# Masking a chunk's last attention unit on VectorE, with its values one step ahead

## The chip, the cores and the metric

The kernel runs on one core of a Trainium2 chip. The metric is the device time of one execution in microseconds, from the median of several runs. The core has five engines that each work through their own queue in order: TensorE (PE, with its weight loads PEld), VectorE (DVE), ScalarE (ACT), GpSimd (POOL) and SyncE (SP), which issues all DMAs of this kernel.

## The reference

Top-k attention for 64 heads, followed by a two-layer MLP with a leaky ReLU:

```python
batch, n_heads, seq, head_dim = (8, 8, 576, 64)
scores = scale * np.matmul(q, k.transpose(0, 1, 3, 2))
kth = np.partition(scores, -32, axis=-1)[..., -32:-31]
scores = np.where(scores >= kth, scores, -1000000000.0)
attn = np.exp(scores - np.max(scores, axis=-1, keepdims=True))
attn = attn / (np.sum(attn, axis=-1, keepdims=True) + 1e-09)
x = np.matmul(attn, v)          # (B,H,S,D) -> (B*S, H*D) = (4608, 512)
h = x @ w_in                    # (512, 2048)
g = np.maximum(0.01 * h, h)
out = g @ w_out                 # (2048, 512)
```

For each query the 32 largest of 576 scores are kept, the others are masked, and what is kept is exponentiated, normalised and multiplied with the values.

## The kernel before, in words

**Units.** The attention is cut into 144 units. A unit is 128 query rows (or two half blocks of 64) of a pair of heads, so it has two score matrices of 128x576. The units of four head pairs together fill 128 tokens. The tokens are cut into chunks for the MLP: two of 128 tokens, then seventeen of 256. Units 0 to 3 make chunk 0, units 4 to 7 chunk 1, units 8 to 15 chunk 2, and so on, eight units each.

**What happens to a unit.** `scores` (L191): PE computes both score matrices into two PSUM tiles `psc0` and `psc1`, ACT copies them into `s_sb`. `top_k` (L209): DVE finds the 32 largest of each row in four rounds of eight, after it has folded the row into maxima and minima of pairs; the round's results go to `tops`, the first entry of the first round is the maximum, the last entry of the last round the threshold. `mask` (L228): POOL computes the bias for the exponential and adds a large negative number to all scores below the threshold. `exponents` (L237): ACT takes the exponential and sums each row into `z`. `sums` (L241): ACT adds 1e-9, giving `ze`. `reciprocals` (L245): DVE. `normalize` (L249): ACT. `transpose` (L252): ACT splits the 32-bit words into two planes of 16 bits (`split`), two DMAs store them to DRAM (`apart`), and a transposing DMA reads them back as `wT`, which has three buffers. `weigh_values` (L276) multiplies with the values on PE into `po`, `keep_values` (L290) copies into the MLP's input `x` on ACT.

**The order.** It is written out by hand, in a loop of steps (L416). In step s DVE does the top k of unit s in four slots (`slot()`); POOL masks unit s-1 and ACT exponentiates it; unit s-2 gets its reciprocals, normalisation and transpose, in the step's second quarter. At every even step the scores of units s+2 and s+3 are made and the values of two units (s-4 and s-3) are weighed, so `values_at(n)` (L356) is n+3, rounded up to an even number. When the values of a chunk's last unit have been weighed, the chunk is ready (`attended`, L373), and its MLP is dealt out in pieces over seven places of each step until the next chunk gets ready (`mlp_steps` and `slot_budget`, L337 and L379). Each MLP piece of the first layer (`ph`) is closed by a Prelu on ACT (L313); three PSUM tiles rotate for both layers. The second layer (`pz`) needs ACT only for one copy per 128 tokens (L326).

**The lead-in.** The MLP weights arrive as 64-bit words in 16 pieces and are rounded to float32 by ACT, DVE and PE together (`round_weights`, L103); a piece goes through three stages in three turns of the loop at L400. The raw pieces lie in the three buffers of the pool `raws`. The scores of units 0 and 1 are issued in this loop too, in the turn of piece 14.

Of the kernel before, what the change touches and what calls it, by code (L numbers as in the profile page):

```python
# [8 lines left out]
F32 = mybir.dt.float32  # L9
U32 = mybir.dt.uint32  # L10
U16 = mybir.dt.uint16
BF16 = mybir.dt.bfloat16
AF = mybir.ActivationFunctionType
ALU = mybir.AluOpType
# [5 lines left out]
def kernel(  # L20
# [13 lines left out]
    nc = tc.nc  # L34
    NPAIR, P, S = qT.shape
# [3 lines left out]
    ROUNDS = TOPK // 8  # L39
    SLOPE = 0.01  # L40
    LOWEST = -3.4028234663852886e38
    SCALE = float(D) ** -0.5
# [5 lines left out]
    WCH = 1024  # L48
# [10 lines left out]
    raws = ctx.enter_context(tc.tile_pool(name="raws", bufs=3))  # L59
    work = ctx.enter_context(tc.tile_pool(name="work", bufs=2))  # L60
    small = ctx.enter_context(tc.tile_pool(name="small", bufs=5))
# [18 lines left out]
    NPIECE = 2 * HP * DFF // WCH  # L80
# [13 lines left out]
    def load_weights(n):  # L94
        if n >= NPIECE:
            return
        if not AS_WORDS:
            nc.sync.dma_start(piece(n), weights[n])
            return
        raw_of[n] = raws.tile([P, WCH, 4], U16, name="raw")  # L100
        nc.sync.dma_start(raw_of[n].rearrange("p n w -> p (n w)"), weights[n])
# [51 lines left out]
    def load_qk(pi):  # L153
        qt = loads.tile([P, S], F32, name="qt")
        kt = loads.tile([P, S], F32, name="kt")
        nc.sync.dma_start(qt, qT[pi])
        nc.sync.dma_start(kt, kT[pi])
        qk_of[pi] = qt, kt

    def load_v(pi):  # L160
        v_of[pi] = loads.tile([P, NKC, 2, D], F32, name="vt", bufs=LOADED_V)
        nc.sync.dma_start(v_of[pi], vk[pi])
# [28 lines left out]
    def scores(u):  # L191
        ps = [ps_sc.tile([P, 2, 512], F32, name=f"psc{i}") for i in range(2)]
        for n in range(0, len(u.parts), 2):
            for half in range(2):
                for i, pi, side, r0 in u.parts[n:n + 2]:
                    qt, kt = qk_of[pi]
                    d = slice(side * D, (side + 1) * D)
                    nc.tensor.matmul(  # L198
                        ps[i][r0:r0 + u.rows, half, 0:HS],
                        qt[d, u.q0:u.q0 + u.rows],  # L200
                        kt[d, half * HS:(half + 1) * HS],
                        start=True, stop=True,
                    )
        u.both = work.tile([P, 2, S], F32, name="s_sb", bufs=5)
        u.s = [u.both[:, i, :] for i in range(2)]
        for i in range(2):
            nc.scalar.copy(u.s[i].rearrange("p (h n) -> p h n", h=2), ps[i][:, :, 0:HS])  # L207

    def top_k(u):  # L209

        u.tops = small.tile([P, 2, ROUNDS, 8], F32, name="tops")
        pairs = work.tile([P, 2, 2, HS], F32, name="pairs", bufs=1)
        for n, op in enumerate((ALU.max, ALU.min)):
            nc.vector.tensor_tensor(pairs[:, :, n, :], u.both[:, :, 0:HS], u.both[:, :, HS:S], op)  # L216
        for r in range(ROUNDS):
            rest = [pairs[:, i, 0, :] if r < ROUNDS // 2 else
                    pairs[:, i, :, :].rearrange("p n h -> p (n h)") for i in range(2)]
            for i in range(2):  # L220
                nc.vector.max(out=u.tops[:, i, r, :], in_=rest[i])  # L221
            if r + 1 < ROUNDS:
                for i in range(2):
                    nc.vector.match_replace(out=rest[i], in_to_replace=u.tops[:, i, r, :],  # L224
                                            in_values=rest[i], imm_value=LOWEST)
            yield

    def mask(u, i):  # L228
        if i == 0:
            u.nbias = small.tile([P, 2], F32, name="nbias")  # L230
            u.z = small.tile([P, 2], F32, name="z")
            nc.gpsimd.tensor_scalar(u.nbias, u.tops[:, :, 0, 0], -SCALE, None, ALU.mult)  # L232
        pen = work.tile([P, S], F32, name="pen", bufs=1)
        nc.gpsimd.tensor_scalar(pen, u.s[i], u.tops[:, i, ROUNDS - 1, 7:8], MASKED, ALU.is_lt, ALU.mult)  # L234
        nc.gpsimd.tensor_tensor(u.s[i], u.s[i], pen, ALU.add)  # L235
# [5 lines left out]
    def sums(u):  # L241
        u.ze = small.tile([P, 2], F32, name="ze")
        nc.scalar.activation(u.ze, u.z, AF.Copy, bias=1e-9, scale=1.0)  # L243

    def reciprocals(u):  # L245
        u.rz = small.tile([P, 2], F32, name="rz")
        nc.vector.reciprocal(u.rz, u.ze)  # L247

    def normalize(u, i):  # L249
        nc.scalar.activation(u.s[i], u.s[i], AF.Copy, bias=0.0, scale=u.rz[:, i:i + 1])  # L250

    def transpose(u):  # L252


        pairs = u.both.rearrange("p i n -> p (i n)").bitcast(U16).rearrange("p (n h) -> p n h", h=2)
        apart = halves.tile([P, 2, 2 * S], U16, name="apart")
        for h in range(2):
            split = work.tile([P, 2 * S], U16, name="split", bufs=2)
            nc.scalar.copy(split, pairs[:, :, h])  # L259
            nc.sync.dma_start(apart[:, h, :], split)  # L260
        u.wT = work.tile([P, 2 * NKC - 1, P], F32, name="wT", bufs=3)
        nc.sync.dma_start_transpose(out=u.wT.bitcast(U16), in_=apart.rearrange("p h n -> (p h) n"))
# [89 lines left out]


    LAG = 3

    def values_at(n):  # L356

        return n + LAG + (n + LAG) % 2

    steps = units  # L360

    def unit(n):
        return steps[n] if 0 <= n < len(steps) else None
# [15 lines left out]
    def slot_budget(s):  # L379

        after = [at for at, _ in ready_at if at >= s]
        until = after[0] if after else s
        return backlog[0] / ((until + 1 - s) * SLOTS)
# [3 lines left out]
    with tc.manual_schedule():  # L387
        last = {p: n for n, u in enumerate(steps) for p in u.pairs}

        def load_more(s):  # L390

            for of, load, n, lag in ((qk_of, load_qk, LOADED, -2), (v_of, load_v, LOADED_V, LAG + 1)):
                while len(of) < NPAIR and (len(of) < n or last[len(of) - n] + lag <= s):
                    load(len(of))


        for n in range(3):
            load_weights(n)
        rounding = {}
        for n in range(NPIECE + 2):  # L400
            for i in (n, n - 1, n - 2) if AS_WORDS else ():
                if 0 <= i < NPIECE:
                    if i == n:
                        rounding[i] = round_weights(i)
                    next(rounding[i], None)
            load_weights(n + 3)
            if 6 <= n < 6 + HP:
                load_qk(n - 6)
            elif n == NPIECE - 2:
                for u in steps[0:2]:  # L410
                    scores(u)
            elif n == NPIECE - 1:
                load_v(0)
                load_v(1)

        for s in range(len(steps) + LAG + 1):  # L416
            cur, old, older, new = unit(s), unit(s - 1), unit(s - 2), ()
            if s % 2 == 0:
                new = [u for u in steps[s + 2:s + 4] if u]
            picks = top_k(cur) if cur else iter(())  # L420
            budget = slot_budget(s)

            def slot():
                next(picks, None)

            slot()
            if old:
                mask(old, 0)
                mask(old, 1)
            mlp_steps(budget)  # L430
            slot()
            if older:
                reciprocals(older)
                normalize(older, 0)
                normalize(older, 1)
            mlp_steps(budget)
            if old:
                exponents(old, 0)
            if older:
                transpose(older)  # L440
            slot()
            mlp_steps(budget)
            mlp_steps(budget)
            slot()
            mlp_steps(budget)
            if old:
                exponents(old, 1)
                sums(old)
            for u in new[:1]:
                scores(u)  # L450
            if s % 2 == 0:
                po = ps_po.tile([P, 2, P], F32, name="po")
                for values in (weigh_values, keep_values):
                    for n, u in enumerate((unit(s - LAG - 1), unit(s - LAG))):
                        if u:
                            values(u, po[:, n, :])
                attended(s)
            for u in new[1:]:
                scores(u)
            budget = slot_budget(s + 1)  # L460
            mlp_steps(budget)
            mlp_steps(budget)
            load_more(s)
        mlp_steps(1e9)
# [58 lines left out]
```

## Time and profile before

| | |
|---|---|
| median of three runs | 1515.37 us (1514.73 to 1516.42) |
| profiled execution, span | 1512.57 us, 1510.8 us |
| PE busy | 1423.4 us (94%) |
| DVE busy | 1330.6 us (88%) |
| ACT busy | 1117.7 us (74%) |
| POOL busy | 1078.1 us (71%) |
| mask on POOL, L234 and L235 | 288 times each, 2214 and 1411 ns |
| exponential, L238 | 288 times, 768 ns |
| split, L259 | 288 times, 1144 ns |
| tensor_tensor of 128x576 on DVE, L216 | 288 times, 780 ns |

Times in the profile are microseconds from the start of the span. An engine's busy time is what its instructions took; a bracket such as [6.15 <-DMA wT<-apart] behind an instruction is the idle time before it and what ended that. "x20" is the number of instructions that a line merges. A line number is that of the kernel before.

### The profile page before, as it was taken

Reading aid. Unit: us, or ns where it says so; the run is one execution under the profiler, and the core shown is the slowest. Engines: PE = TensorE matmul, PEld = TensorE weight load, DVE = VectorE, ACT = ScalarE, POOL = GpSimd, SP = SyncE. Lnnn points to the kernel's source line nnn. Section 1 sums busy time; section 2 is a strip of 40 time slices with the busy share of each in tenths; the row PEclk is TensorE's granted clock in tenths of the full one; section 3 lists DMA queues with packets and bytes.
Section 4 is the critical chain, followed back from the end, with each engine's and each line's share of the span. In section 5 each row is a group of like instructions: output and inputs, shape, how many; then the busy total and the mean of one; then the engine's idle time right before and its main releaser. Section 6 shows DMA issues by size and latency. Waiting matters only on the chain.

```text
span 1510.8 us, 24439 instructions
## 1 busy us (share of the span) xinstructions
PE 1423.4 (94%) x8190; PEld 946.7 (63%) x8192; DVE 1330.6 (88%) x3421; ACT 1117.7 (74%) x2141; POOL 1078.1 (71%) x726
## 2 busy tenths in 40 slices
PE   5736978999999999999999999999999999999998
PEld 2214655767676766676767666767666666676774
DVE  6799999999899999899999998999999989999600
ACT  7846787878787877787878787878787777787720
POOL 0058878887777877777778787878887878788700
PEclk9966999999999999999999999999999999999999
DMA  7714466555665455545764455645665455554510
GB/s 284 283 31 126 131 173 167 162 140 144 183 158 154 128 158 163 169 128 153 181 169 136 140 159 166 170 133 145 188 162 146 133 159 154 152 136 140 141 50 14
DMA packets 399294, 227.05 MB, mean 150 GB/s; under 512 B 343360, under 2 KB 343360, under 8 KB 397120
## 3 DMA queue, kind: packets, MB, share of 16 engines
q1 hardware_dynamic: 399168, 225.49, 53.4%
q8 instruction: 64, 1.05, 0.3%
q14 instruction: 62, 0.51, 0.1%
HBM read 46.14 MB, written 94.37 MB: 93 GB/s over the span
## 4 chain that ended last, share of the span: by engine, by line
PE 83%; DVE 10%; ACT 4%; DMA 1%; issue 1%; POOL 0%; DVEq 0%; ACTq 0%; POOLq 0%
PE pz L319 32%; PE ph L307 31%; PE psc L198 10%; PE po L283 10%; DVE tops L221 4%; DVE pairs L224 3%; DVE pairs L216 1%; ACT split L259 1%; DMA wT<-apart 1%; DMA raw<-in_weights_dram 1%; ACT s_sb L238 1%; ACT s_sb L250 0%; DVE scale L144 0%; ACT s_sb L207 0%; ACT wT L121 0%
## 5 line engine op out<-in xcount | busy, mean ns | idle before, releaser
L234 POOL TENSOR_SCALAR pen<-s_sb,tops 128x576 f32<-128x576 f32 x288 | 637.5, 2214 | 234.4 <-DVE tops L221 197.4
L221 DVE MAX8 tops<-pairs 128x8 f32<-128x288 f32 (+1 forms) x1152 | 636.1, 591 | 0.0
L307 PE MATMUL ph<-x,w_in 128*128 128x256 f32 (+1 forms) x2432 | 515.4, 371 | 6.4 <-ACT gT L313 6.4
L319 PE MATMUL pz<-w_out,gT 128*128 128x512 f32 x1152 | 506.8, 595 | 1.3 <-ACT gT L313 1.3
L307 PEld LDWEIGHTS ph<-x,w_in 128*128 128x128 f32 x2432 | 440.5, 191 | 86.5 <-issue 21.5
L224 DVE MATCH_REPLACE8 pairs<-tops,pairs 128x288 f32<-128x288 f32 (+1 forms) x864 | 460.3, 538 | 0.0
L235 POOL TENSOR_TENSOR s_sb<-s_sb,pen 128x576 f32<-128x576 f32 x288 | 406.5, 1411 | 24.1
L319 PEld LDWEIGHTS pz<-w_out,gT 128*128 128x128 f32 x1152 | 216.0, 190 | 265.9 <-issue 263.5
L259 ACT COPY split<-s_sb 128x1152 uint16<-128x1152 uint16 x288 | 315.6, 1144 | 0.0
L207 ACT COPY s_sb<-psc 128x576 f32<-128x576 f32 x288 | 169.2, 639 | 114.1 <-PE psc L198 114.1
L250 ACT ACTIVATE s_sb<-s_sb,rz 128x576 f32<-128x576 f32 x288 | 206.6, 767 | 33.7 <-DVE rz L247 33.6
L238 ACT ACTIVATE s_sb<-s_sb,nbias 128x576 f32<-128x576 f32 x288 | 221.1, 768 | 11.4 <-POOL s_sb L235 11.4
L198 PE MATMUL psc<-kt,qt 64*128 64x288 f32 (+1 forms) x1280 | 198.1, 439 | 28.5 <-ACT s_sb L207 28.4
L216 DVE TENSOR_TENSOR pairs<-s_sb 128x576 f32<-128x576 f32 x288 | 213.6, 780 | 10.2 <-ACT s_sb L238 0.5
L283 PE MATMUL po<-wT,vt 128*64 128x128 f32 (+1 forms) x3200 | 180.5, 269 | 21.1 <-DMA wT<-apart 21.0
L283 PEld LDWEIGHTS po<-wT,vt 128*64 128x64 f32 x3200 | 161.6, 139 | 52.6 <-issue 27.2
L313 ACT ACTIVATE gT<-ph 128x256 f32<-128x256 f32 (+1 forms) x304 | 107.1, 368 | 97.8 <-PE ph L307 97.4
L198 PEld LDWEIGHTS psc<-kt,qt 64*128 64x128 f32 (+1 forms) x1280 | 110.1, 181 | 100.9 <-ACT s_sb L207 37.8
L232 POOL TENSOR_SCALAR nbias<-tops 128x2 f32<-128x2 f32 x144 | 33.4, 232 | 92.3 <-DVE tops L221 79.6
L247 DVE RECIPROCAL rz<-ze 128x2 f32<-128x2 f32 x144 | 22.4, 156 | 70.0 <-ACT ze L243 69.4
L297 ACT COPY x<-po 128x128 f32<-128x128 f32 (+1 forms) x160 | 32.4, 264 | 63.4 <-PE po L283 63.4
L224 DVE MATCH_VALUE_LOAD pairs<-tops,pairs 128x8 f32 x864 | 62.6, 72 | 0.0
(38 smaller groups left out, 312.2 us busy)
## 6 DMA issues: line engine op xcount, KB each, us to landing
apart<-split SPq DMA_DIRECT2D x288, 288.0 KB, 2.1
raw<-in_weights_dram SPq DMA_DIRECT2D x16, 1024.0 KB, 4.9
vt<-in_vk_dram SPq DMA_DIRECT2D x32, 320.0 KB, 3.6
qt<-in_qT_dram SPq DMA_DIRECT2D x32, 288.0 KB, 4.0
kt<-in_kT_dram SPq DMA_DIRECT2D x32, 288.0 KB, 4.2
out_dram<-o_sb SPq DMA_DIRECT2D x36, 256.0 KB, 2.0
wT<-apart SPq DMA_TRANSPOSE x144, 4.6
```

What stands on the lines that cost most here:

```text
L198: nc.tensor.matmul(ps[i][r0:r0 + u.rows, half, 0:HS], qt[d, u.q0:u.q0 + u.rows], kt[d, half * HS:(half + 1) * HS], start=True, stop=True,)
L216: nc.vector.tensor_tensor(pairs[:, :, n, :], u.both[:, :, 0:HS], u.both[:, :, HS:S], op)
L221: nc.vector.max(out=u.tops[:, i, r, :], in_=rest[i])
L224: nc.vector.match_replace(out=rest[i], in_to_replace=u.tops[:, i, r, :], in_values=rest[i], imm_value=LOWEST)
L234: nc.gpsimd.tensor_scalar(pen, u.s[i], u.tops[:, i, ROUNDS - 1, 7:8], MASKED, ALU.is_lt, ALU.mult)
L235: nc.gpsimd.tensor_tensor(u.s[i], u.s[i], pen, ALU.add)
L238: nc.scalar.activation(u.s[i], u.s[i], AF.Exp, bias=u.nbias[:, i:i + 1], scale=SCALE, accum_out=u.z[:, i:i + 1])
L250: nc.scalar.activation(u.s[i], u.s[i], AF.Copy, bias=0.0, scale=u.rz[:, i:i + 1])
L259: nc.scalar.copy(split, pairs[:, :, h])
L283: nc.tensor.matmul(po[side * D:(side + 1) * D, o, :], vt[:, c, side, :], u.wT[:, c + side * NKC if c + 1 < NKC else c, r:r + n], start=(c ...
L307: nc.tensor.matmul(ph[:, 0:n], w_in[c][:, f * P:(f + 1) * P], x[c][:, 0:n], start=(c == 0), stop=(c == HP - 1),)
L319: nc.tensor.matmul(pz[0:m, 0:DMODEL], gT[f][:, r0:r0 + m], w_out[f // 4][:, f % 4, :], start=(f == 0), stop=(f == NFC - 1),)
```

## The change

It concerns the last unit of each of the first five chunks: units 3, 7, 15, 23 and 31, called hurried here. For them the exponentials of all 576 scores, not of the masked ones, are taken on ACT during the unit's own step, as soon as the first round of its top k has given the maximum; they go into a buffer of the pool `raws`, which is free by then. At the head of the next step DVE masks and sums them in one instruction per matrix: (score >= threshold) times exponential, with a row sum. Then the reciprocals, the normalisation and the transpose are issued for the unit before it and for the hurried unit, one after the other, ahead of the step's top k. POOL does nothing for a hurried unit. The values of it and of the unit before are weighed one step earlier, in an odd step, so the chunk is ready one step earlier.

Apart from that, the scores of units 0 and 1 are issued one turn later in the lead-in, in the turn of piece 15.

```diff
+    def hurried_exponents(u):
+        u.nbias = small.tile([P, 2], F32, name="nbias")
+        nc.scalar.activation(u.nbias, u.tops[:, :, 0, 0], AF.Copy, bias=0.0, scale=-SCALE)
+        e = raws.tile([P, WCH, 4], U16, name="raw").rearrange("p n w -> p (n w)").bitcast(F32)
+        u.e = [e[:, i * S:(i + 1) * S] for i in range(2)]
+        for i in range(2):
+            nc.scalar.activation(u.e[i], u.s[i], AF.Exp, bias=u.nbias[:, i:i + 1], scale=SCALE)
+
+    def hurried_masks(u):
+        u.z = small.tile([P, 2], F32, name="z")
+        for i in range(2):
+            nc.vector.scalar_tensor_tensor(
+                out=u.s[i], in0=u.s[i], scalar=u.tops[:, i, ROUNDS - 1, 7:8], in1=u.e[i],
+                op0=ALU.is_ge, op1=ALU.mult, accum_out=u.z[:, i:i + 1])
+        u.ze = small.tile([P, 2], F32, name="ze")
+        nc.vector.tensor_scalar(u.ze, u.z, 1e-9, None, ALU.add)
...
+    HURRIED = {3, 7, 15, 23, 31}
     def values_at(n):
-        return n + LAG + (n + LAG) % 2
+        return n + LAG + (n + LAG) % 2 - ((n | 1) in HURRIED)
...
-            elif n == NPIECE - 2:
+            elif n == NPIECE - 1:
                 for u in steps[0:2]:
                     scores(u)
-            elif n == NPIECE - 1:
+            if n == NPIECE - 1:
                 load_v(0)
                 load_v(1)
...
+            if s - 1 in HURRIED:
+                hurried_masks(old)
+                for u in (older, old):
+                    reciprocals(u)
+                for u in (older, old):
+                    normalize(u, 0)
+                    normalize(u, 1)
+                    transpose(u)
+                old = older = None
+            elif s - 2 in HURRIED:
+                older = None
             slot()
+            if s in HURRIED:
+                hurried_exponents(cur)
...
-            if s % 2 == 0:
+            due = [u for n, u in enumerate(steps) if values_at(n) == s]
+            if due:
                 po = ps_po.tile([P, 2, P], F32, name="po")
                 for values in (weigh_values, keep_values):
-                    for n, u in enumerate((unit(s - LAG - 1), unit(s - LAG))):
-                        if u:
-                            values(u, po[:, n, :])
+                    for n, u in enumerate(due):
+                        values(u, po[:, n, :])
                 attended(s)
```

## The prediction

> **What bounds the kernel now.** I read the page's forty slices first, then the stages, then the timelines of PE, DVE and ACT over the first 260 us.
>
> ```profile
> PE   5736978999999999999999999999999999999998
> DVE  6799999999899999899999998999999989999600
> ```
> PE is short of work in the first seven slices only (one slice is 37.8 us); DVE is full there. The stages say it in numbers (columns: stage, length, then busy time of PE, PEld, DVE, ACT, POOL, and PE clock):
> ```profile
> 80.00:145.00 65.00, 26.62 (x137) 18.29 (x135) 64.55 (x173) 35.96 (x67) 49.95 (x34) 0.56 0.30 84
> 145.00:192.00 47.00, 42.22 (x298) 31.19 (x297) 44.20 (x116) 35.32 (x75) 39.23 (x27) 0.99 0.46 121
> 192.00:255.00 63.00, 50.76 (x393) 34.27 (x394) 61.28 (x161) 50.44 (x106) 50.24 (x35) 0.95 0.65 177
> 410.00:490.00 80.00, 80.00 (x438) 54.62 (x437) 73.99 (x193) 63.56 (x126) 62.80 (x43) 1.00 0.59 151
> 490.00:1440.00 950.00, 949.48 (x5594) 639.04 (x5593) 876.63 (x2282) 739.75 (x1449) 748.01 (x499) 1.00 0.56 152
> ```
> From 255 us to the end PE never rests, so the end moves only by PE idle time that is removed or added early on. Up to there DVE sets the pace: a step of top k takes 8.87 us (rows of L216 below), and DVE waits for nothing but this:
> ```profile
> 113.88 1.45 DVE L216 TENSOR_TENSOR pairs<-s_sb 128x576 f32<-128x576 f32 x2
> 122.68 1.52 DVE L216 TENSOR_TENSOR pairs<-s_sb 128x576 f32<-128x576 f32 x2
> ...
> 154.52 0.17 DVE L247 RECIPROCAL rz<-ze 128x2 f32<-128x2 f32 x1 [0.58 <-ACT ze L243]
> ...
> 192.90 0.17 DVE L247 RECIPROCAL rz<-ze 128x2 f32<-128x2 f32 x1 [2.73 <-ACT ze L243]
> ...
> 223.85 1.45 DVE L216 TENSOR_TENSOR pairs<-s_sb 128x576 f32<-128x576 f32 x2
> ```
> These are the starts of steps 4, 5 and 16. PE in turn waits for the transposed weights of a chunk's last unit (po), and the MLP (ph) starts behind them:
> ```profile
> 138.94 2.40 PE L283 MATMUL po<-wT,vt 128*64 128x128 f32 x20 [6.15 <-DMA wT<-apart]
> 142.20 2.82 PE L198 MATMUL psc<-kt,qt 64*128 64x288 f32 x8 [0.85 <-ACT s_sb L207]
> 144.95 6.23 PE L307 MATMUL ph<-x,w_in 128*128 128x128 f32 x48
> ...
> 249.94 2.40 PE L283 MATMUL po<-wT,vt 128*64 128x128 f32 x40
> 253.00 1.77 PE L198 MATMUL psc<-kt,qt 64*128 64x288 f32 x8 [0.65 <-ACT s_sb L207]
> 254.70 10.65 PE L307 MATMUL ph<-x,w_in 128*128 128x256 f32 x48
> ```
> The first group is unit 3 and chunk 0; the second units 14 and 15 and chunk 2, after which PE is saturated. Unit 3's top k ends at 113.8, its weights are there at 138.9: 25.1 us.
>
> [...]
>
> **The change, part by part.**
> *Mask.* Per hurried unit two DVE passes of 128x576: from 0.71 us each (L216 in pairs)[...]; I take 0.76. With two accumulator reads (about 0.1 each) and ze this is 1.65 us[...]. POOL loses its 7.2 us of L234 and L235; it is not the bound.
>
> *Exponentials early.* ACT gains nbias (0.2) and moves two exponentials (1.44 as a pair) ahead of the normalisation and exponentials of the step. So the sum ze of the unit before comes 1.65 us later.
>
> *Reciprocals first.* In before DVE asks for ze of the unit two back 4.5 us into a step (118.40 in step 4). Now it asks at the head of the step, behind the masks. All of the step's top k queues behind that wait, and by it PE's scores and POOL's masks. This is the price I find decisive. h is what a hurried unit delays DVE:
> - Unit 3: ACT copies scores until 110.24 (109.06+1.18), then exponentials to 111.9, then the old sequence from normalise to ze, 5.3 us (110.14 to 115.43): ze at 117.2. The masks are done at 115.5[...]. Two reciprocals, 0.3: step 4 starts at 117.6, not 113.88. h=3.7.
> - Unit 7: chunk 0's MLP now runs in steps 6 and 7, so ACT also carries its Prelus. Step 6 starts at 135.1, normalise follows the reciprocal at 139.7-140.3, ze of unit 5 at 146.1 (5.8 us as in the rows at 156.38 to 162.15, Prelus in between); two score copies with PE between them to 149.6, two Prelus to 150.4, exponentials to 152.0, normalise to ze again 5.8 with some more Prelus: 158.5. DVE would have been there at 152.8. h=5.7 (5 to 7.5).
> - Unit 15: ACT is free at 220.1 (behind the score copy of 218.86), so by the old rows ze of unit 14 moves from 225.7 to 227.4, 3.6 after the step's start at 223.85; with reciprocals h=3.9.
> - Units 23 and 31: second half of a chunk, where pz needs no Prelu; I take 3.5 each.
>
> *The chain to the weights.* From the reciprocals on: normalise and split of one unit 1.44+2.19, the same of the other: 7.2 us of ACT. SP is in order: the first transpose is issued 2.2 us after its split, holds SP 2.5, the second unit's apart DMAs come behind it, 3.3 us later its transpose, 4.6 to landing. For unit 3: 117.5, splits done 121.1 and 124.7, transposes at 123.3 and 129.3, weights at 133.9. That is 20.1 us after top k's end, 5.0 less than before. wT has three buffers, so unit 7's transpose also waits until PE has weighed unit 4's values, by my count at 168, before the transpose's own time of 170.4 (158.8+11.6); not a new bound, but close.
>
> *Values one step ahead.* Chunk 0's MLP starts at 137 instead of 145, but scores of units 8 and 9 (2.8 each at the slow clock) now stand behind it. What counts is the start of chunk 2, where PE fills up. Step 16 starts at 223.85 + 3.7 + 5.7 - 3.3 (DVE's two waits above, which the shift swallows) = 229.9. Weights of unit 15 at +20.1 = 250.0, po 1.3, copy 0.3: MLP at 251.6. Two scores of step 18 (2.4 us) are still to do, so it compares as 254.0 with 254.7: 0.7 us gained.
>
> *Scores one piece later in the lead-in.* ACT starts on piece 15 2.8 us earlier (71.86 to 69.1), but four score copies and PE's scores now stand ahead of the scale of piece 15 (74.97 to 75.9) and its matmuls: DVE ends at 79.0 instead of 78.6. 0.4 lost, between 1 gained and 1.5 lost.
>
> *Back to the old rhythm.* Chunks 3 and 4 take PE 74.6 us for eight steps (po of 325.28 to 399.86); DVE needs 71 plus h. The chunk after the last hurried unit has nine steps between its values: PE 77.1. PE is done at 251.6+74.6+74.6+77.1 = 477.9. DVE: step 40 at 229.9+213+10.9 (h of 15, 23, 31) = 453.8, weights of unit 39 by the old chain at +25.1 = 478.9. PE waits 1.0.
>
> Sum: -0.7+0.4+1.0 = 0.7 us slower, against the span of 1510.8. The profiled run took 1512.57, the median of the timed ones is 1515.37; I add to the latter: 1516.0.
>
> **Rivals.**
> *Slower: DVE becomes the bound for the hurried chunks.* For: 71+3.5 is already 74.5 against PE's 74.6, and where PE lags, ze waits for PE through ACT's queue (46 waits of 69.4 us in the whole of before). If h of 15, 23 and 31 sum to 16 instead of 10.9, unit 39's weights come at 484, PE waits 6: 1521. It decides from a sum of about 13. Against: in these steps ACT has few Prelus.
> *Faster: the sums are there in time.* If unit 6's sum comes with the masks' end (h=2 at unit 7), chunk 2 starts 4.4 us ahead; with later h summing to 9.9 or less PE doesn't wait at unit 39, and 0.4 goes for the lead-in: 1511.4. For: ACT is 74% busy only; against: its order in steps 6 and 7 as worked out. All waits gone, h=1.9 everywhere, brings step 16 5.6 us forward and shortens its chain by 1.7: 1507.8.
> *The chain is not shortened.* If SP's order costs the whole 5 us (qk loads before the transpose, as at 230 us, where 5 us passed between apart and transpose), chunk 2 is 4 us late: 1520. It is counted with slower.
>
> **How the numbers follow.** No change from before can be told within 0.2%, that is 3.0 us. Level 0.37 (own range 1512.4 to 1518.4), slower 0.35 (1518.4 to 1527), faster 0.28 (1507.8 to 1512.3). The bounds of the parts (h of unit 7 5 to 7.5, lead-in, later h) spread by some 4 us each way, and the rivals by 6; leaving out a tenth at each end gives 1508 to 1525.
>
> **What would show it.** Right: chunk 0's first ph near 137; a DVE wait for ze at the head of steps 4, 8 and 16 of about 2, 4 and 2 us; the pair of transposes some 6 us apart; chunk 2's first ph near 252; a po wait near 478. Wrong: reciprocals there without a wait (faster), masks above 1.4 us each so that they outlast ze, PE idle at each of the chunk starts at 326 and 401 (slower), or top k beginning well before 78 or after 80.

## The result and the profile after

The changed kernel takes 1539.31 us (median of 4 runs, 1537.61 to 1542.27) against 1515.35 for the kernel before: ratio 1.0159, 95% interval 1.0141 to 1.0178. It is 24 us slower. The forecast was 1516.0, with a range up to 1525: too low. The rival "VectorE becomes the bound for the hurried chunks" points the right way, but the loss is four times as large as it has it.

The forty slices of the page are too coarse to show the loss. The stages show it (stage, length, busy time of PE, PEld, DVE, ACT and POOL, PE clock). The kernel before:
```profile
255.00:330.00 75.00, 74.94 (x495) 50.79 (x494) 73.98 (x193) 58.66 (x118) 62.74 (x43) 1.00 0.63 158
330.00:410.00 80.00, 80.00 (x441) 54.74 (x440) 75.95 (x200) 62.38 (x122) 64.42 (x43) 1.00 0.57 159
```
The changed kernel:
```profile
255.00:330.00 75.00, 72.10 (x479) 49.34 (x479) 64.95 (x170) 56.36 (x112) 46.24 (x31) 0.98 0.49 137
330.00:410.00 80.00, 75.80 (x416) 50.59 (x415) 73.93 (x196) 58.24 (x112) 53.93 (x38) 1.00 0.54 140
490.00:1440.00 950.00, 948.64 (x5584) 640.91 (x5583) 892.96 (x2326) 739.89 (x1452) 755.76 (x505) 1.00 0.56 152
```
In 255 to 330 us DVE is busy for 65 of 75 us, where it had 74, and PE now rests in stages in which it never rested. From 490 us on PE is full in both. So the loss is made between units 3 and 40, as the times of each chunk's first MLP matmul show, read off PE's timelines:

| first ph of chunk | before | after | difference |
|---|---|---|---|
| 0 | 144.95 | 136.83 | -8.1 |
| 1 | 186.72 | 185.44 | -1.3 |
| 2 | 254.70 | 261.55 | +6.9 |
| 3 | 330.60 | 342.74 | +12.1 |
| 4 | 405.19 | 424.83 | +19.6 |
| 5 | 480.55 | 505.59 | +25.0 |

Chunk 0 does start 8 us earlier, as forecast (137). Most of the gain is gone at chunk 1, and each of the chunks 2 to 5 loses 5 to 8 us more. The largest part, 18.2 of the 25 us, comes between the starts of chunk 2 and chunk 5, where PE had been full. This stretch in the kernel before, then in the changed one:
```profile
254.70:480.55 225.85, 225.79 (x1330) 152.39 (x1330) 216.19 (x564) 176.25 (x347) 182.78 (x123) 1.00 0.60 158
261.55:505.59 244.04, 235.09 (x1347) 156.86 (x1346) 223.86 (x586) 182.61 (x356) 170.66 (x115) 0.99 0.54 147
```
PE is idle for 8.9 us of it, where it had no idle time, and busy for 9.3 us more. About 2.5 of these 9.3 us are two scores that now fall into the stretch instead of ahead of it.

VectorE's timeline of after, at the heads of steps 4, 8 and 16:
```profile
113.52 0.80 DVE L265 SCALAR_TENSOR_TENSOR s_sb<-s_sb,tops,raw 128x576 f32<-128x576 f32 x1
114.25 0.08 DVE L265 DVE_READ_ACCUMULATOR s_sb<-s_sb,tops,raw 128x1 f32 x1
...
116.86 0.23 DVE L247 RECIPROCAL rz<-ze 128x2 f32<-128x2 f32 x2 [1.59 <-ACT ze L243]
117.01 1.41 DVE L216 TENSOR_TENSOR pairs<-s_sb 128x576 f32<-128x576 f32 x2
...
153.59 0.82 DVE L265 SCALAR_TENSOR_TENSOR s_sb<-s_sb,tops,raw 128x576 f32<-128x576 f32 x1 [1.40 <-ACT raw L259]
...
160.09 0.23 DVE L247 RECIPROCAL rz<-ze 128x2 f32<-128x2 f32 x2 [4.72 <-ACT ze L243]
...
237.17 0.23 DVE L247 RECIPROCAL rz<-ze 128x2 f32<-128x2 f32 x2 [2.76 <-ACT ze L243]
...
283.50 0.17 DVE L247 RECIPROCAL rz<-ze 128x2 f32<-128x2 f32 x1 [4.74 <-ACT ze L243]
```
The masks cost about what was taken. The forecast waits for ze are there, 1.59, 4.72 and 2.76 us for about 2, 4 and 2. Two rows show waits that were not forecast: at 153.59 the masks of unit 7 wait 1.40 us for the early exponentials (raw), and in step 20, four steps behind the masks of unit 15, VectorE waits 4.74 us at the reciprocal's usual place.

What stands behind unit 15, on ACT, on PE and on SP:
```profile
247.91 2.21 ACT L278 COPY split<-s_sb 128x1152 uint16<-128x1152 uint16 x2 [5.52 <-DMA apart<-split]
```
```profile
239.61 1.22 PE L198 MATMUL psc<-kt,qt 64*64 64x288 f32 x16
...
250.70 2.84 PE L198 MATMUL psc<-kt,qt 64*64 64x288 f32 x16 [3.92 <-ACT s_sb L207]
```
```profile
238.32 2.46 SPq L281 DMA_TRANSPOSE wT<-apart  x1
...
243.70 0.86 SPq L279 DMA_DIRECT2D apart<-split  x2
248.58 2.63 SPq L281 DMA_TRANSPOSE wT<-apart  x1
251.31 1.01 SPq L279 DMA_DIRECT2D apart<-split  x2
254.69 2.49 SPq L281 DMA_TRANSPOSE wT<-apart  x1
```
The three transposes are unit 13's, 14's and 15's. Behind the first, SP issues four loads of queries and keys (240.88 to 243.60) before unit 14's planes. ACT has only two split buffers, so unit 15's splits wait 5.52 us for them, the copies of the next scores come behind that, and PE, with MLP work in hand, stands 3.92 us in front of a score matmul. The scores behind it then take 2.84 us instead of 1.22.

PE's clock adds to that: in this trace it falls behind some of PE's pauses. The granted clock goes from 1.00 to 0.50 at 244.1 us, within a wait of 2.31 us (242.07 to 244.38) and before the 3.92 us begin, and stays there until 254.3. It falls again for 3.4 us at 271.4, just behind a wait of 2.10 us, and at 411.3, behind one of 3.02. One of these stretches, and one with a wait of 1.45 us at 349.83, in which the clock stayed full:
```profile
271.50:274.70 3.20, 3.20 (x9) 2.08 (x7) 3.10 (x6) 1.28 (x2) 2.08 (x3) 0.50 0.82 184
348.00:352.00 4.00, 2.56 (x14) 1.41 (x11) 4.00 (x14) 3.11 (x8) 3.82 (x3) 1.00 0.37 133
```
Over the whole span PE's idle time grew by 12.1 us (87.4 to 99.5, span less busy time), and its busy time by 13.3 us (1423.4 to 1436.7) for the same matmuls. PE is busy at half clock for 57.5 us in the changed kernel and for 34.9 before; half of the difference, 11 us, is an estimate of what the clock adds to the busy time, with work at half clock put at twice as long (20 matmuls of values took 2.40 us at 244.38, at half clock, and 1.31 at 240.76, at full). (In the run with nothing hurried, below, it gives 5.0 us where PE was busy for 4.4 us longer, at no loss of time.) Not all of it is lost: most of it lies ahead of chunk 2, where PE still has idle time. Of the 18.2 us between chunks 2 and 5 the clock explains 3.4 at most (half of the two stretches of 3.4 us).

### The profile page after: what moved, and what is told of

The parts are those of the page before. It is cut to its first block, busy times and chain, and to the rows that moved or that the text cites. A ratio compares the mean times of both kernels' runs of the same rounds, so it can differ in the third digit from the quotient of the medians.

```text
span 1536.2 us, 24433 instructions
## 1 busy us (share of the span) xinstructions
PE 1436.7 (94%) x8190; PEld 954.3 (62%) x8192; DVE 1338.4 (87%) x3446; ACT 1117.6 (73%) x2131; POOL 1040.5 (68%) x701
## 4 chain that ended last, share of the span: by engine, by line
PE 80%; ACT 8%; DVE 6%; DMA 3%; issue 1%; SPq 0%; DVEq 0%; ACTq 0%
PE pz L338 30%; PE ph L326 30%; PE psc L198 10%; PE po L302 9%; ACT split L278 3%; DVE tops L221 2%; DVE pairs L224 2%; ACT s_sb L250 1%; ACT s_sb L238 1%; DMA apart<-split 1%; DMA wT<-apart 1%; DMA raw<-in_weights_dram 1%; DVE pairs L216 1%; ACT s_sb L207 1%; ACT wT L121 1%
## 5 line engine op out<-in xcount | busy, mean ns | idle before, releaser
L234 POOL TENSOR_SCALAR pen<-s_sb,tops 128x576 f32<-128x576 f32 x278 | 615.4, 2214 | 255.4 <-DVE tops L221 217.9
L235 POOL TENSOR_TENSOR s_sb<-s_sb,pen 128x576 f32<-128x576 f32 x278 | 392.2, 1411 | 23.2
L238 ACT ACTIVATE s_sb<-s_sb,nbias 128x576 f32<-128x576 f32 x278 | 213.6, 768 | 19.1 <-POOL s_sb L235 19.1
L216 DVE TENSOR_TENSOR pairs<-s_sb 128x576 f32<-128x576 f32 x288 | 213.3, 779 | 9.7 <-DVE tops L221 0.5
L345 ACT COPY o_sb<-pz 128x512 f32<-128x512 f32 x36 | 21.1, 585 | 58.1 <-PE pz L338 58.1
```

Source lines behind the costliest of these rows:

```text
L238: nc.scalar.activation(u.s[i], u.s[i], AF.Exp, bias=u.nbias[:, i:i + 1], scale=SCALE, accum_out=u.z[:, i:i + 1])
```

## The experiments

All figures are against the kernel before, in the same series of runs; the interval in brackets is that of the ratio. The theory after the result: **two waits**, VectorE waiting at a hurried step's head for the sum of the unit before (A), and PE and ACT asked for the values a step too early (B). The rivals: the split buffers and SP's order (C), the lead-in (D), the masks' own work (E). Every run in which a unit is hurried has E in it, so A is never seen without E.

**Masks only**: the change with the old places of the values.
```diff
-        return n + LAG + (n + LAG) % 2 - ((n | 1) in HURRIED)
+        return n + LAG + (n + LAG) % 2
```


> The change without its step ahead: the five units get their exponentials early, their masks on VectorE and their reciprocals, normalisation and transposes at the head of the next step, but the values stay at the even steps of before. If DVE's wait for the sum of the unit before (25.5 us of delay at five step heads in the changed kernel, of which 9 are the masks' own work) is the cause by itself, chunks get ready as late as DVE is: about 1539, perhaps more, for the step gained is missing. If the cause is that PE and, behind it, ACT stand at values that are asked for a step too early, the waits of PE for po go and the time falls to about 1520.

Measured: 1541.31 us, ratio 1.0174 (1.0159 to 1.0189). As slow as the whole change, without the step ahead. Step 16 starts at 242 instead of 224 and chunk 2 at 274.4, 20 us late: A together with E is enough. How much of it E has is seen below, where both waits are gone.

**Values only**: the kernel before with the five odd steps and no other edit.
```diff
+    HURRIED = {3, 7, 15, 23, 31}
-        return n + LAG + (n + LAG) % 2
+        return n + LAG + (n + LAG) % 2 - ((n | 1) in HURRIED)
...
+            due = [u for n, u in enumerate(steps) if values_at(n) == s]
...
```


> Before, with the values of the last two units of the first five chunks one step earlier, and nothing else: masks stay on POOL. The weights are there 25 us after the end of top k and PE asks after about 18, so PE should wait some 7 us at each of the five places. If asking early is the main cause, this is as slow as the change or slower: 1535 to 1545. If DVE's delays are the cause, only what PE loses in the stages where it is full counts (units 23 and 31, and a part of 15), against a step gained: 1515 to 1525.

Measured: 1550.63 us, 1.0242 (1.0222 to 1.0262). PE, ACT and VectorE of this run at unit 15's values:
```profile
265.12 2.40 PE L283 MATMUL po<-wT,vt 128*64 128x128 f32 x20 [5.38 <-DMA wT<-apart]
```
```profile
267.56 0.43 ACT L297 COPY x<-po 128x128 f32<-128x128 f32 x2 [8.74 <-PE po L283]
```
```profile
275.98 0.17 DVE L247 RECIPROCAL rz<-ze 128x2 f32<-128x2 f32 x1 [5.76 <-ACT ze L243]
```
ACT stands at the copy of values that PE has not made, and the sums queue behind it; at the values of units 3 and 23 VectorE waits 5.63 and 7.53 us in the same way. So B too is enough by itself, and it reaches VectorE. This is B at its hardest, for here the weights come no earlier than in before.

**Reciprocals late**: the unit before keeps its old place, so nothing is waited for at the head.
```diff
-                for u in (older, old):
-                    reciprocals(u)
-                for u in (older, old):
-                    normalize(u, 0)
-                    normalize(u, 1)
-                    transpose(u)
-                old = older = None
+                reciprocals(old)
+                normalize(old, 0)
+                normalize(old, 1)
+                transpose(old)
+                old = None
```


> The change, but at the head of the step only the hurried unit is handled; the unit before it gets its reciprocals, normalisation and transpose at its old place in the second quarter of the step. So DVE waits at the head for nothing that ACT does, and ACT's eight operations in a row become two groups of four. If DVE's wait for ze is the cause, the five delays fall from 25.5 us to about 10 and the time to about 1520 or less. If the order on SP and the two split buffers are the cause, the same four splits in a row are gone too, and the same gain comes, with the waits of split for apart gone; the run with more split buffers tells them apart. If asking for values a step early is the cause, little changes: above 1533.

Measured: 1543.44 us, 1.0186 (1.0164 to 1.0208). A alone would have given 1520: missed. The waits did go from the heads (steps 3, 15, 23 and 31 take 10.6 us with the masks; in step 7 the masks still wait 2.92 us for the exponentials), but came back at the usual place of the reciprocals:
```profile
194.63 0.17 DVE L247 RECIPROCAL rz<-ze 128x2 f32<-128x2 f32 x1 [5.88 <-ACT ze L243]
...
368.39 0.17 DVE L247 RECIPROCAL rz<-ze 128x2 f32<-128x2 f32 x1 [6.10 <-ACT ze L243]
```
With A gone, B and E cost as much. The edit also turns the order of the two units round, but at unit 15 the last transpose of the pair still goes out 22.3 us after top k's end (258.34 against 236.00; 22.0 us in the change), so B is about as hard here as there.

**Both gone**: reciprocals late and the old places of the values together.

> Neither of the two waits: the hurried unit alone is handled at the head of the step, the unit before it keeps its old place, and the values keep their even steps. If the wait for ze at the head and the values asked for a step early are two causes, each enough by itself, then this one, which has neither, costs no more than the masks' own work on VectorE, five times 1.9 us, less what PE's fullness hides: 1516 to 1525. If a third thing (the early exponentials on ACT, the moved scores) is behind all the slow runs, it stays above 1533.

Measured: 1531.3 us, 1.0109 (1.0096 to 1.0122): 16 us slow instead of 24, outside both expectations. Two waits remain that are before's own, grown from 2.73 us (step 12) and 2.83 (step 36):
```profile
198.89 0.17 DVE L247 RECIPROCAL rz<-ze 128x2 f32<-128x2 f32 x1 [5.43 <-ACT ze L243]
...
432.17 0.17 DVE L247 RECIPROCAL rz<-ze 128x2 f32<-128x2 f32 x1 [6.28 <-ACT ze L243]
```
E is thus not the 9 us of its own rows only. VectorE starts step 40 18.9 us later than in before: five times 1.75 us, 8.8 in all, are the masks' rows, and about 10 are waits for ze that have grown, these two and those of steps 20 and 34 above all. A part of C stands behind them: at units 3, 15, 23 and 31 ACT waits 1.60, 5.43, 1.56 and 3.97 us for the split buffers, which it never does in before, and at units 15 and 31 PE waits for ACT behind that. Unit 31:
```profile
396.41 2.21 ACT L278 COPY split<-s_sb 128x1152 uint16<-128x1152 uint16 x2 [3.97 <-DMA apart<-split]
```
```profile
399.21 2.82 PE L198 MATMUL psc<-kt,qt 64*128 64x288 f32 x8 [3.33 <-ACT s_sb L207]
```
PE is 12.2 us later than before at the values ahead of this place (393.47 against 381.26) and 18.9 at the first ones behind it (418.79 against 399.86). This kernel with more split buffers was not run, so how much of its 16 us is C's is open.

**Split buffers and loads**: splits of a hurried unit in a raw buffer, the loads behind its transposes.
```diff
+        own = None
+        if hasattr(u, "e"):
+            own = raws.tile([P, WCH, 4], U16, name="raw").rearrange("p n w -> p (n w)")
         for h in range(2):
-            split = work.tile([P, 2 * S], U16, name="split", bufs=2)
+            if own is not None:
+                split = own[:, h * 2 * S:(h + 1) * 2 * S]
+            else:
+                split = work.tile([P, 2 * S], U16, name="split", bufs=2)
...
+                load_more(s - 1)
...
-            load_more(s)
+            if s not in HURRIED:
+                load_more(s)
```


> The change, with two split buffers of its own for the hurried unit (in the pool of the raw weights), and the loads of queries and keys that are due at the end of a hurried unit's step issued behind the two transposes instead of ahead of them. DVE still waits for ze at the head. If ACT's wait for the split buffers (11.4 us at five places, 5.5 at unit 15) and the score copies and PE behind it are the cause, the time falls by 10 us or more, to 1529 or less. If DVE's wait for ze is the cause, it falls by some 2 to 5 us only.

Measured: 1547.12 us, 1.0204 (1.0184 to 1.0225). The edit made a new wait, of PE for the keys it had delayed, so it tells little on C:
```profile
261.13 2.18 PE L198 MATMUL psc<-kt,qt 64*64 64x288 f32 x8 [11.66 <-DMA kt<-in_kT_dram]
```

**Split buffers alone**, the first part of that edit:

> The change with two split buffers of its own for each hurried unit, and the loads left in their place (in the run with both edits PE waited 11.7 us for late keys). If ACT's wait for the split buffers (5.5 us at unit 15, 11.4 in all) is on the path, 5 us or more faster than the change: 1534 or less. If ACT stands elsewhere for longer anyway, within 3 us of the change: 1536 to 1542.

Measured: 1540.42 us, 1.0167 (1.015 to 1.0185). ACT's waits for the buffers are gone from the list of waits, and no time with them; at unit 15's values PE now waits 4.31 us for the weights instead. So the buffers alone are not what makes the change slow while A and B are in it. That does not clear them beside A and B (see the run with both gone), and SP's order alone was not tried without harm to the keys.

**Nothing hurried**: `HURRIED = set()`, so that only the moved scores are left.

> No unit is hurried; of the change only the scores of units 0 and 1 in the turn of the last weight piece are left. The changed kernel's first top k began 0.17 us earlier than before's, so the same time within 0.1%: 1514 to 1517. If the lead-in carries a cost that the other runs share, it shows here.

Measured: 1514.95 us, 1.0001 (0.9993 to 1.0009). D falls.

**Single units**, the set reduced to one member each:

> Only unit 3 is hurried (chunk 0). VectorE loses 3.5 us at the head of step 4 and PE gets its first MLP work 8 us earlier, but PE is short of work later, until chunk 2, and then that delay is what counts: slower by 1 to 5 us. If the values asked for early are what costs, ACT and PE wait for each other in steps 5 to 12, and it is slower by 5 to 9 us. Faster only if the 8 us are kept.

> Only unit 7 is hurried (chunk 1). If the delay of VectorE at the head of the next step is what a hurried unit costs ahead of PE's fullness, this is the dearest of the early ones (8 us at that head in the changed kernel): slower by 4 to 8 us. If the places were just added up from what is measured (-3 for unit 3, +4 for unit 15, +24 for all five), units 7, 23 and 31 together owe 23 us, some 8 each.

> Only unit 15 is hurried (chunk 2, behind which PE is full). Nothing delays VectorE before step 16; the chain to unit 15's weights is some 5 us shorter. By the prediction's sum chunk 2 then starts 3 to 5 us earlier in PE's own count and the kernel gains that: 1510 to 1513. If the order on SP (second transpose behind loads) and the two split buffers eat the chain's gain, and the step after the values in the odd step costs waits, it is slower by 5 us or more: above 1520.

> Only unit 23 is hurried, in the stage where PE never rests in the kernel before. Nothing can be gained there, since PE has no idle time to fill. If a hurried unit costs only what VectorE loses, PE's backlog hides it: within 2 us of before. If the values in an odd step, the second transpose and the nine steps that follow make PE wait even here, it is slower by 4 us or more, with PE idle in 255 to 410 us and its clock lowered behind the waits.

> Only unit 31 is hurried, late in the stage where PE never rests. By what unit 23 showed alone (its chunk a step earlier, then nine steps that took 82 us instead of 77): 1 to 5 us slower than before, 1516 to 1520.

| hurried | median us | ratio (95%) |
|---|---|---|
| 3 | 1512.0 | 0.9982 (0.9975 to 0.9989) |
| 7 | 1530.67 | 1.0104 (1.0091 to 1.0118) |
| 15 | 1519.27 | 1.0031 (1.0021 to 1.0042) |
| 23 | 1516.68 | 1.0010 (1.0001 to 1.0019) |
| 31 | 1519.27 | 1.0033 (1.0020 to 1.0045) |

With unit 23 alone PE was idle for 1.45 of the 80 us from 330 to 410, and its granted clock was 0.98 there.

Unit 3 alone is faster than the kernel before, by 2.9 us; I had expected it slower. PE's timeline: its chunk's MLP starts at 137.3 and chunk 2 at 256.75 with scores 20 and 21 done.
```profile
137.30 2.93 PE L326 MATMUL ph<-x,w_in 128*128 128x128 f32 x12
...
256.75 3.50 PE L326 MATMUL ph<-x,w_in 128*128 128x256 f32 x15
```
Chunk 0 is ready in step 5 and chunk 1, as in before, in step 10, so chunk 0's MLP has five steps instead of four. The gain is only a third of the 7.7 us by which that chunk starts earlier, and in this one profiled execution chunk 2 starts no earlier than before (254.70), so where the gain lies can't be read from it.

Unit 7 alone costs two thirds of the whole. PE, ACT and DVE there:
```profile
174.07 12.18 PE L338 MATMUL pz<-w_out,gT 128*128 128x512 f32 x28
```
```profile
188.63 0.43 ACT L316 COPY x<-po 128x128 f32<-128x128 f32 x2 [11.91 <-PE po L302]
```
```profile
196.51 0.17 DVE L247 RECIPROCAL rz<-ze 128x2 f32<-128x2 f32 x1 [9.06 <-ACT ze L243]
```
Chunk 0's MLP starts where it did before (144.8) but must be dealt out in three steps instead of four. PE does its rest ahead of the values (174.07 to 186.25), ACT stands 11.91 us at their copy, and VectorE, which sets the pace here, 9.06 us behind ACT. In the whole change chunk 0 is a step ahead as well and keeps its four steps: there the same copy waits 6.68 us (at 183.74) and VectorE 0.36 and 1.31 in steps 11 and 12.

**Unit 7, values weighed at the head of the odd step**, ACT's copy left in its place:
```diff
+            due = [u for n, u in enumerate(steps) if values_at(n) == s]
+            early = due and s % 2 == 1
+            if early:
+                po = ps_po.tile([P, 2, P], F32, name="po")
+                for n, u in enumerate(due):
+                    weigh_values(u, po[:, n, :])
...
-                for values in (weigh_values, keep_values):
+                for values in (keep_values,) if early else (weigh_values, keep_values):
```


> Unit 7 alone, as in the run of that name (16 us slower), but in its odd step 9 PE weighs the values at the head of the step, ahead of the five places where the rest of chunk 0's MLP is dealt out; ACT's copy of them into x stays where it was in ACT's queue. If the 16 us come from ACT standing 11.9 us at that copy behind PE's MLP work (and VectorE 9.1 us behind ACT), the copy finds its values some 6 to 9 us earlier and the time falls by 5 us or more, to 1525 or less. If they come from VectorE's wait at the head of step 8 (7.3 us), it stays at 1529 to 1531.

Measured: 1529.2 us, 1.0090 (1.0075 to 1.0105), no difference that can be told from unit 7 alone. ACT:
```profile
180.36 0.43 ACT L316 COPY x<-po 128x128 f32<-128x128 f32 x2 [3.33 <-PE po L302]
...
190.84 0.58 ACT L345 COPY o_sb<-pz 128x512 f32<-128x512 f32 x1 [10.05 <-PE pz L338]
```
The copy gets its values 8 us earlier, and ACT stands at the next copy instead, for the end of the same MLP work. So it isn't the values' copy: what is next in ACT's queue waits for PE, which has a fourth step's MLP to do in three.

**Unit 7, old place of the values:**

> Unit 7 alone, with its values at the even step of before. VectorE's 7 us at the head of step 8 are left, the odd step is gone. If the odd step is the larger part of the 16 us, 1519 to 1523; if the head is, 1527 or more.

Measured: 1523.19 us, 1.0054 (1.0035 to 1.0073). Of unit 7's 16 us half goes with B, the odd step. The other half is A together with E, which this run does not part.

**Units 3 and 15, with reciprocals late:**

> Only unit 3 is hurried, and unit 2 keeps its old place, so VectorE doesn't wait for unit 2's sum at the head of step 4: 1.7 us less delay of VectorE than with unit 3 alone. VectorE sets the pace up to chunk 2, so by the wait theory 1 to 2 us faster than that: 1510 to 1511. If the delay at the head doesn't matter, 1512 as there.

> Only unit 15 is hurried, and unit 14 keeps its old place. The hurried unit is then first in SP's queue, ahead of unit 14, and the head of step 16 has no wait of 1.9 us. If these two are what costs there, 4 us or more faster than unit 15 alone (1519): 1515 or less. If the odd step of the values is what costs, still 1518 to 1522.

Measured: 1512.91 us, 0.9989 (0.9980 to 0.9997), and 1519.35 us, 1.0034 (1.0022 to 1.0047). The head's wait taken away buys nothing at either: it is not the head alone.

**Sets of units:**

> The change for units 3, 15, 23 and 31, without unit 7. From the single runs (unit 3: 3 us faster, 7: 16 slower, 15: 4 slower, 23: 2 slower) against 24 for all five, it should be 6 to 10 us slower than before, 1521 to 1525, if the costs add. If units hurried one after another wear VectorE's lead down and that is the cause, it is not much better than the change: above 1530.

> Units 23 and 31 hurried, two chunks in a row. If what counts is the stretch from one hurried chunk to the next (81 to 83 us for eight steps in the changed kernel and without unit 7, against 74.6), because with the values a step earlier VectorE, ACT and PE wait for one another in a ring with no step to spare, this pair costs 6 us more than the two units alone: 1523 to 1529. If the units' costs add, 1517 to 1521.

Measured: 1539.19 us, 1.0153 (1.0122 to 1.0183) for 3, 15, 23 and 31; 1524.67 us, 1.0072 (1.0058 to 1.0086) for 23 and 31. The costs don't add: the four cost as much as the five, and the four singles sum to 8.5. From one hurried chunk to the next, eight steps take 81.2 and 82.1 us in the change, 83.5 and 82.5 without unit 7 and 81.1 with 23 and 31 (first ph to first ph), against 75.9 and 74.6 in before. Two hurried chunks in a row cost about 4 us beyond their singles (10.9 against 6.5 by the ratios, with intervals that nearly reach it).

## Why the prediction was wrong

- Bound, lead-in and masks: right. The masks took 0.80 us and 0.08 for the accumulator (0.76 and 0.1 taken), 1.75 us in all. The terms as listed add up to about 1.9 and not to the 1.65 that was written; nothing hangs on it. The first top k began 0.17 us earlier where 0.4 later was forecast, hidden in a time that did not change.
- Waits at the head: right in kind and place, undersized. h was 3.5, 8.0, 4.7, 4.1 and 5.2 (step's end to the next top k) against 3.7, 5.7, 3.9, 3.5 and 3.5. At unit 7, 1.40 of the 8.0 us is the masks' wait for the early exponentials, which the sum did not have. The three late ones sum to 14.0; the rival named 13 as its point of decision.
- The chain to the weights: right for unit 3 (134.64 against 133.9), wrong for unit 15, whose transpose went out at 254.69, 22.0 us after top k's end at 232.65, where the sum has 15.5. The rival "the chain is not shortened" named the loads in SP's order; the sum left them out, and missed that ACT has two split buffers for four splits.
- **The step that failed is what stands behind the values one step ahead**, in two terms of the sum. "Values one step ahead" has chunk 2's MLP begin at 251.6, and it began at 261.55. "Back to the old rhythm" has 227.3 us from there to chunk 5 (74.6, 74.6, 77.1 and a wait of 1.0), and it took 244.0. Both count PE's work and VectorE's heads, and put no price on ACT, which copies values, scores and hidden activations in one order and stands wherever PE is late, with the next units' sums behind it. One step earlier for the values takes 8.9 us from the distance between VectorE and PE, of which the shorter chain gives back 5 at best and the masks' heads take 4 again.
- What this did to VectorE can be added up. It started step 40 at 473.8 us, where the sum has 453.8. Of these 20 us, 2.8 were there at the end of unit 15's top k (232.65 against 229.9), 3.1 are what the three later heads took above the forecast, and 14.5 are seven waits for ze at the reciprocal's usual place, in steps 18 to 36, that "71 plus h" puts at nothing, although before already has about 8 us of such waits between steps 16 and 40. In the last odd step ACT stood 8.07 us at the copy of the values (at 423.13), and VectorE waited 2.38 us for the sum that came behind it (at 431.38, in step 35). So the three chunks took 81.2, 82.1 and 80.8 us.
- How far it is shown: the values alone make the kernel 36 us slower without any other part of the change. The heads with the masks make it 26 slower, of which the masks without both waits have 16. At unit 7 the odd step is half. That PE, ACT and VectorE wait for one another in turn is read from the timelines; no run shows it apart.
- Still open: how much of the 16 us with both waits gone is the split buffers', and why the sets don't add.

## What to carry to other kernels

In a pipeline of in-order queues, a step that is pulled ahead takes its distance away from every engine whose queue passes it: price the copy behind it, and what stands behind that copy, before counting the gain. A gain belongs where the pace-setting engine and the late one have room between them; here that was only the first chunk, and the hurry for it alone is worth 0.2%. Where several waits each suffice, taking one away can show nothing, so test them apart and together, and test a rival again where the main causes are gone.

## What the runs showed of the hardware

A scalar_tensor_tensor of 128x576 in float32 with both tensors in SBUF, a per-partition scalar and an accumulator output took 0.80 us in the changed kernel (L265), and the read of the accumulator 0.08, against a median of 0.752 for a tensor_tensor of the same size in the kernel before (L216). And PE's granted clock fell to one half behind pauses of 2.10, 2.31 and 3.02 us in the changed kernel, for at least 3.4 us each time. Behind a pause of 1.45 us it stayed full there (at 349.83), and in the kernel before also behind pauses of 2.36 (at 191.92) and 2.53 us (at 198.74), so these runs give no length from which it falls. A short wait of a full PE could thus cost more than its own length: at 250.70, at half clock, sixteen score matmuls took 1.6 us more than at full clock (2.84 against 1.22 at 239.61).
